# A weight decode whose low part is subtracted on GpSimd instead of TensorE and ScalarE, with a new table of issue times

## The chip, the cores and the metric

The kernel runs on one core of one Trainium2 chip. The metric is device time in microseconds (us) of one execution, from the launch to the last output. Five engines work on their own instruction streams, each in order: PE (TensorE, matrix products), DVE (VectorE, elementwise), ACT (ScalarE, activation functions and copies), POOL (GpSimd, elementwise here), and SP (SyncE), which only issues the DMA transfers. They wait for each other through semaphores.

## What is computed

Two layers, one behind the other. The first is a recurrent attention (an mLSTM) over 4 batches, 8 heads, 768 positions and a head size of 40:

```python
for t in range(S):
    m_new = np.maximum(f_gate[:, :, t] + m, i_gate[:, :, t])
    f_stab = np.exp(f_gate[:, :, t] + m - m_new)
    i_stab = np.exp(i_gate[:, :, t] - m_new)
    m = m_new
    C = f_stab[..., None, None] * C + i_stab[..., None, None] * np.einsum('bhd,bhe->bhde', vt, kt)
    n = f_stab[..., None] * n + i_stab[..., None] * kt
    h_tilde = np.einsum('bhde,bhe->bhd', C, qt)
    denom = np.maximum(np.abs(np.einsum('bhd,bhd->bh', n, qt)[..., None]), 1.0)
    y[:, :, t] = sigmoid(o_gate[:, :, t]) * h_tilde / denom
```

The second is a feed-forward layer on the 3072 tokens of 320 features: `h = x @ w_in`, `g = h * erf(softplus(h))`, `out = g @ w_out`, with 2048 hidden features. The two weight matrices reach the device as 64-bit floats.

## The kernel before

**Attention in chunks.** The 768 positions are cut into 6 chunks of 128, and each chunk of each batch is one of 24 steps (`attention(s)`, line 497). A step makes gate products on PE (L566, L568), their exponential on ACT (`dm`, L573), a causal mask of `dm` on POOL (`affine_select`, L577, 128x512), scores on PE (L586 or L589), their product with the mask on DVE (L600), outputs and state (L626, L629, L639, L645, L652), the division by the denominator (L666 to L669), a small copy on POOL that fills a third block of 128 columns (L672), and three transposes (L678). The result goes to `xh` (ACT, L687) and `xl` (DVE, L691): the high part that a single-pass float matmul keeps, and the rest.

**The feed-forward layer in groups.** `mlp(g)` (line 801) is called for 48 groups. Each has 32 "up" matmuls into `h` (L818), nine instructions on ACT (L828 to L859, and `gh`, L868), four on DVE (L851, L855, L863, and L873, which makes `gl`, what `gh` leaves over), and 24 "down" matmuls: 16 with `gh` (L887, L888) and 8 with `gl` (L890). Four groups belong to two steps. L873 is the last elementwise pass of a group, and the group's eight L890 read it.

**Weights.** They are not loaded as floats but decoded on the chip. `decode` (line 699) is called 26 times: 10 blocks of 128x512 from `w_in` (two of them, the tails, put together from rows 256 to 319) and 16 blocks of 128x320 from `w_out`. ACT takes the upper word of each 64-bit number (`val`, L707), DVE shifts and merges bits in three passes (`bits`, L712, L713, L715), ACT writes the high part `hi` (`wh` or `woh`, L720), and the low part is `val - hi`: PE makes the difference in PSUM with two matmuls against the identity and the negative identity (`dif`, L725 and L726), and ACT copies it to `wl` or `wol` (`lo`, L730). For the tails, `lo` ends with `done()`: four DMA issues (L775) that put its halves in place in `wh`. `val` lies in a pool named `moe` that has two buffers of the name `bits`, so the third decode waits until the first has read its `val` for the last time. `raw` words of `w_out` lie in the two buffers `parts`, three blocks in each.

**What sets the order.** Each unit of work (a step, a group, a decode, a load) has a start time, and each of its parts an offset, from tables at the top of the file. `plan` is sorted by start plus offset, and the parts are written out in that order. So the tables set the order in which each engine, the DMA queue of SP among them, gets its instructions. The numbers in them are only sort keys.

The difference that the change touches is made by these lines:

```python
@at('dif')
def _():
    v.z = ps_a.tile([128, 512], F32, name="pa")[:, 0:n]
    nc.tensor.matmul(v.z, ident, v.val, start=True, stop=False)
    nc.tensor.matmul(v.z, nident, hi(), start=False, stop=True)
@at('lo')
def _():
    nc.scalar.activation(lo(), v.z, AF.Copy)
```

Of the kernel before, what the change touches and what calls it, by code (L numbers as in the profile page):

```python
# [49 lines left out]
SETUP = {'setup': -653.6399, 'rhs0': -316.5197, 'rhs1': -7.8928, 'sel': -20.425}  # L50
GATE = {'load': -160.6071,
    'scan': -129.7377,
    'g': -118.9644,
    'sum': -85.9459,
    'exp': -69.3145,
    'part0': -64.8632,
    'part1': -57.829,
    'part2': -53.3066,
    'rhs': -44.557}
ATT_FIRST = {'load': -98.3436,  # L60
    'loadv': -167.9076,
    'khi': -0.958,
    'qhi': -84.1108,
    'klo': -36.0204,
    'qlo': -40.8927,
    'stk0': -106.1734,
    'stk1': -42.28,
    'rows': -205.5,
    'pe0': -204.9951,
    'pe1': -84.7223,  # L70
    'ex0': -104.2074,
    'ex1': -80.6796,
    'sel0': -99.9161,
    'sel1': -76.6928,
    'S0': -72.5713,
    'S1': -66.4977,
    'vg0': -86.1606,
    'vg1': -75.2945,
    'w0': -66.7387,
    'w1': -60.3516,  # L80
    'th': -51.6975,
    'pq': -84.6914,
    'qa': -69.7526,
    'ph0': -50.833,
    'ph1': -48.4014,
    'ph2': -41.1641,
    'ph3': -34.4417,
    'pk0': -76.6612,
    'pk1': -43.5318,
    'sa0': -34.523,  # L90
    'sa1': -33.2596,
    'sk0': -75.5148,
    'sk1': -41.374,
    'den': -25.7622,
    'yg': -25.29,
    'y': -21.6911,
    'tr': -15.7542,
    'xh': -3.4201,
    'xl': -0.3588}
ATT_NEXT = {'load': -108.5865,  # L100
    'loadv': -65.7264,
    'khi': -43.9486,
    'qhi': -36.8481,
    'klo': 33.0974,
    'qlo': 4.1048,
    'stk0': -62.7653,
    'stk1': 33.0459,
    'rows': -112.0,
    'pe0': -92.4353,
    'pe1': -82.6231,  # L110
    'ex0': -85.3469,
    'ex1': -74.7973,
    'sel0': -83.8594,
    'sel1': -59.1013,
    'S0': -64.4044,
    'S1': -29.3249,
    'vg0': -46.0099,
    'vg1': -19.402,
    'w0': -39.4592,
    'w1': -14.1493,  # L120
    'th': -41.0893,
    'pq': -109.6295,
    'qa': -38.5364,
    'ph0': -10.0541,
    'ph1': -6.3375,
    'ph2': 5.1946,
    'ph3': 6.4602,
    'pk0': -35.9301,
    'pk1': -7.3506,
    'sa0': 27.0234,  # L130
    'sa1': -6.4202,
    'sk0': -34.6458,
    'sk1': -0.3263,
    'den': 17.2106,
    'yg': 28.411,
    'y': 30.5578,
    'tr': 34.3008,
    'xh': 35.0968,
    'xl': 36.9102}
ATT = {'load': -38.0873,  # L140
    'loadv': -22.0289,
    'khi': -26.4131,
    'qhi': -24.304,
    'klo': -21.0673,
    'qlo': -20.9744,
    'stk0': -13.01,
    'stk1': -20.7116,
    'rows': -35.0,
    'pe0': -16.191,
    'pe1': -27.6979,  # L150
    'ex0': -14.5235,
    'ex1': -17.8549,
    'sel0': -13.8199,
    'sel1': -15.9236,
    'S0': -5.8456,
    'S1': -11.6692,
    'vg0': -8.7917,
    'vg1': -11.6286,
    'w0': -5.765,
    'w1': -10.6719,  # L160
    'th': -5.5334,
    'pq': -27.7455,
    'qa': -20.3849,
    'ph0': 1.4564,
    'ph1': 1.6614,
    'ph2': 2.8445,
    'ph3': 3.6732,
    'pk0': 6.9497,
    'pk1': -1.5624,
    'sa0': 7.8642,  # L170
    'sa1': 7.8309,
    'sk0': 10.4729,
    'sk1': 17.4327,
    'den': 7.2966,
    'yg': 10.4519,
    'y': 11.8501,
    'tr': 12.5049,
    'xh': 15.9467,
    'xl': 18.6409}
DEC = {'val': 5.0509, 'bits': 10.1649, 'hi': 15.9164, 'lo': 23.6056, 'dif': 16.8262}  # L180
MLP_FIRST = {'up0': -25.2675,
    'up1': -24.8742,
    'up2': -13.1693,
    'up3': -10.2026,
    'hb0': -14.0725,
    'a0': -9.4604,
    'hb1': -7.0234,
    'a1': -0.5942,
    'a2': 7.0246,
    'sq': 10.8333,  # L190
    'b': 13.8647,
    'ah': 14.2406,
    'ab': 17.9958,
    'w': 25.3005,
    'wh': 30.591,
    'gh': 34.499,
    'gl': 42.3954,
    'dn0': 37.1922,
    'dn1': 48.9497,
    'dn2': 59.2234,  # L200
    'dn3': 64.3577,
    'dn4': 42.875,
    'dn5': 45.5271,
    'dn6': 49.4724,
    'dn7': 59.5752,
    'o0': 36.8732,
    'o1': 34.0907}
MLP_NEXT = {'up0': -18.4874,
    'up1': -16.4563,
    'up2': -11.6119,  # L210
    'up3': -8.3726,
    'hb0': -3.5817,
    'a0': -3.1283,
    'hb1': 1.554,
    'a1': 4.6412,
    'a2': 9.7819,
    'sq': 14.1995,
    'b': 19.2975,
    'ah': 18.6881,
    'ab': 23.8216,  # L220
    'w': 27.514,
    'wh': 30.5244,
    'gh': 31.6065,
    'gl': 34.1835,
    'dn0': 38.7502,
    'dn1': 41.4674,
    'dn2': 41.7867,
    'dn3': 43.0183,
    'dn4': 38.1388,
    'dn5': 38.505,  # L230
    'dn6': 38.8279,
    'dn7': 41.0082,
    'o0': 45.1806,
    'o1': 52.9655}
MLP = {'up0': 10.8805,
    'up1': 11.4884,
    'up2': 11.8654,
    'up3': 11.9285,
    'hb0': 15.2244,
    'a0': 15.6598,  # L240
    'hb1': 17.0074,
    'a1': 18.439,
    'a2': 21.5715,
    'sq': 26.4364,
    'b': 28.2508,
    'ah': 28.025,
    'ab': 31.1556,
    'w': 32.9184,
    'wh': 36.5709,
    'gh': 37.7529,  # L250
    'gl': 40.6316,
    'dn0': 53.5649,
    'dn1': 53.9605,
    'dn2': 62.3419,
    'dn3': 63.3041,
    'dn4': 58.6761,
    'dn5': 59.5966,
    'dn6': 64.956,
    'dn7': 65.2067,
    'o0': 65.5077,  # L260
    'o1': 71.0278}
MLP_END = {'up0': 2.8495,
    'up1': 12.452,
    'up2': 10.3409,
    'up3': 12.5617,
    'hb0': 14.7709,
    'a0': 14.8932,
    'hb1': 15.2803,
    'a1': 16.0175,
    'a2': 20.7093,  # L270
    'sq': 21.7587,
    'b': 24.9917,
    'ah': 35.3148,
    'ab': 39.3943,
    'w': 173.4526,
    'wh': 195.2319,
    'gh': 199.4465,
    'gl': 241.5957,
    'dn0': 241.7219,
    'dn1': 242.5048,  # L280
    'dn2': 242.974,
    'dn3': 247.762,
    'dn4': 284.9153,
    'dn5': 289.8658,
    'dn6': 296.6226,
    'dn7': 298.2198,
    'o0': 286.1734,
    'o1': 303.1319}
LOAD = {(0, 0): -100.853,
    (0, 1): -70.8649,  # L290
    (0, 2): -90.992,
    (1, 0): -57.6292,
    (1, 1): -81.5688,
    (2, 0): -81.2243,
    (2, 1): -17.405,
    (1, 2): -88.4947,
    (3, 0): -100.0948,
    (3, 1): -81.2029,
    ('o', 0): -373.8392,
    ('o', 3): -372.7625,  # L300
    ('o', 6): -15.5809,
    ('o', 9): -74.0241,
    ('o', 12): -93.0868,
    ('o', 15): 54.2361}
DECODE = {('i', 0, 0): -96.6206,
    ('i', 0, 1): -36.809,
    ('t', 0): -70.3377,
# [675 lines left out]
```

## Time and profile before

| what | value |
|---|---|
| median of 3 runs | 543.33 us (537.8 to 544.72) |
| the profiled execution's own time | 542.79 us |
| its span, first to last instruction | 541.1 us |
| what lies around the span | 1.7 us |
| TensorE clock granted, mean | 0.987 of full speed |
| DMA | 58.85 MB, mean 109 GB/s |

A row of the page's list of groups gives line, engine, operation, output and inputs, their shapes, count, then busy time in us and the mean of one in ns, then the idle time of the engine just before them and what ended it. A row of the timeline gives start (us from the span's start), duration, engine and line; in square brackets the idle time before it and what ended it. A table of windows gives, for each stretch, the busy time of PE, PEld (weight loads), DVE, ACT and POOL with the number of instructions in brackets, then the granted clock, the DMA share and GB/s.

### The profile page before, as it was taken

Reading aid. Unit: us, or ns where it says so; the run is one execution under the profiler, and the core shown is the slowest. Engines: PE = TensorE matmul, PEld = TensorE weight load, DVE = VectorE, ACT = ScalarE, POOL = GpSimd, SP = SyncE. Lnnn points to the kernel's source line nnn. Section 1 sums busy time; section 2 is a strip of 40 time slices with the busy share of each in tenths; the row PEclk is TensorE's granted clock in tenths of the full one; section 3 lists DMA queues with packets and bytes.
Section 4 is the critical chain, followed back from the end, with each engine's and each line's share of the span. In section 5 each row is a group of like instructions: output and inputs, shape, how many; then the busy total and the mean of one; then the engine's idle time right before and its main releaser. Section 6 shows DMA issues by size and latency. Waiting matters only on the chain.

```text
span 541.1 us, 10846 instructions
## 1 busy us (share of the span) xinstructions
PE 521.8 (96%) x4086; PEld 491.9 (91%) x4086; DVE 435.9 (81%) x693; ACT 448.2 (83%) x714; POOL 92.4 (17%) x112
## 2 busy tenths in 40 slices
PE   3989999999899999999999999999999999999997
PEld 2757799899899999999999999999999999999986
DVE  5987899979788878888888898788898678776663
ACT  5776999989868978979878978878979889889993
POOL 3220001312211211211211211211211220200000
PEclk9996999999899999999999999999999999999999
DMA  8996114504504503404513504513504514400000
GB/s 272 276 324 214 40 34 134 153 27 144 150 2 152 165 25 124 150 16 152 155 35 116 157 17 138 166 38 106 167 8 135 162 44 137 140 1 26 0 25 24
DMA packets 28302, 58.85 MB, mean 109 GB/s; under 512 B 4156, under 2 KB 8764, under 8 KB 28252
## 3 DMA queue, kind: packets, MB, share of 16 engines
q1 hardware_dynamic: 28252, 58.18, 34.8%
q8 instruction: 32, 0.52, 0.4%
q14 instruction: 18, 0.15, 0.1%
HBM read 33.40 MB, written 3.93 MB: 69 GB/s over the span
## 4 chain that ended last, share of the span: by engine, by line
PE 84%; DMA 6%; DVE 4%; ACT 3%; issue 1%; SPq 1%; POOL 0%; DVEq 0%; ACTq 0%; POOLq 0%
PE h L818 32%; PE po L887 10%; PE po L890 10%; PE po L888 9%; PE pa L629 7%; DMA n<-in_w_in_dram 4%; PE pa L626 4%; PE pa L586 3%; PE pa L639 3%; PE pa L725 2%; DMA stk<-parts 2%; PE pa L566 2%; PE pa L678 1%; PE pa L589 1%; SPq L554 1%
## 5 line engine op out<-in xcount | busy, mean ns | idle before, releaser
L818 PE MATMUL h<-xh,wh 128*128 128x256 f32 x576 | 160.1, 287 | 0.0
L818 PE MATMUL h<-xl,wh 128*128 128x256 f32 x576 | 157.3, 282 | 0.0
L887 PE MATMUL po<-woh,gh 128*128 128x320 f32 x384 | 122.4, 330 | 2.1 <-ACT o_sb L896 1.3
L888 PE MATMUL po<-wol,gh 128*128 128x320 f32 x384 | 114.9, 310 | 0.0
L818 PEld LDWEIGHTS h<-xh,wh 128*128 128x128 f32 x576 | 109.6, 190 | 1.9 <-issue 1.0
L818 PEld LDWEIGHTS h<-xl,wh 128*128 128x128 f32 x576 | 109.5, 190 | 0.2
L818 PE MATMUL h<-xh,wl 128*128 128x256 f32 x384 | 108.3, 282 | 0.0
L873 DVE TENSOR_TENSOR gl<-hb,gh 128x1024 fp32r<-128x1024 f32 x48 | 59.7, 1243 | 21.8 <-ACT gh L868 16.6
L577 POOL TENSOR_SCALAR_AFFINE_SELECT dm<-dm 128x512 f32<-128x512 f32 x48 | 47.2, 985 | 170.2 <-ACT dm L573 162.2
L887 PEld LDWEIGHTS po<-woh,gh 128*128 128x128 f32 x384 | 72.8, 190 | 2.7 <-ACT o_sb L896 1.6
L868 ACT ACTIVATE gh<-hb 128x1024 fp32r<-128x1024 f32 x48 | 50.9, 1060 | 28.3 <-DVE hb L863 27.8
L888 PEld LDWEIGHTS po<-wol,gh 128*128 128x128 f32 x384 | 72.9, 190 | 0.6
L818 PEld LDWEIGHTS h<-xh,wl 128*128 128x128 f32 x384 | 73.0, 190 | 0.0
L890 PE MATMUL po<-woh,gl 128*128 128x320 f32 x384 | 72.6, 319 | 0.0
L855 DVE SCALAR_TENSOR_TENSOR n<-n,n 128x1024 f32<-128x1024 f32 x48 | 58.7, 1224 | 14.9 <-ACT n L847 12.2
L851 DVE SCALAR_TENSOR_TENSOR n<-n,hb 128x1024 f32<-128x1024 f32 x48 | 61.8, 1288 | 4.3 <-ACT n L842 4.2
L863 DVE SCALAR_TENSOR_TENSOR hb<-n,hb 128x1024 f32<-128x1024 f32 x48 | 58.4, 1217 | 7.6 <-ACT n L859 7.4
L828 ACT ACTIVATE hb<-h 128x512 f32<-128x512 f32 x96 | 57.3, 597 | 6.1 <-PE h L818 3.3
L859 ACT ACTIVATE n<-n 128x1024 f32<-128x1024 f32 x48 | 51.4, 1070 | 11.4 <-DVE n L855 11.3
L890 PEld LDWEIGHTS po<-woh,gl 128*128 128x128 f32 x384 | 58.9, 188 | 1.1
L834 ACT ACTIVATE n<-h 128x512 f32<-128x512 f32 x96 | 57.8, 602 | 0.0
L629 PE MATMUL pa<-kvo,dm 128*128 128x41 f32 x384 | 54.8, 273 | 0.0
(102 smaller groups left out, 896.4 us busy)
## 6 DMA issues: line engine op xcount, KB each, us to landing
stk<-parts SPq DMA_DIRECT2D x120, 160.0 KB
kvo<-in_kvo_dram SPq DMA_DIRECT2D x24, 484.0 KB
parts<-in_w_out_dram SPq DMA_DIRECT2D x5, 960.0 KB
parts<-in_qk_dram SPq DMA_DIRECT2D x20, 208.0 KB
q_t<-in_qk_dram SPq DMA_DIRECT2D x20, 208.0 KB
out_dram<-o_sb SPq DMA_DIRECT2D x24, 160.0 KB
stk<-in_qk_dram SPq DMA_DIRECT2D x4, 416.0 KB
hb<-in_w_in_dram SPq DMA_DIRECT2D x2, 512.0 KB
```

The costliest lines, as they stand in the source:

```text
L629: nc.tensor.matmul(v.ph[:, 2 * p + j], v.w[j][:, p], v.v1[:, 2 * p + j], start=(c == 0), stop=(c == 0 or j == 1))
L818: nc.tensor.matmul(v.h[n // 2][:, n % 2 * T:(n % 2 + 1) * T], w, m, start=(q == 0), stop=(q == len(ops) - 1))
L828: nc.scalar.activation(v.hb[:, hs], v.h[i], AF.Copy)
L834: nc.scalar.activation(v.a[:, hs], v.h[i], AF.Tanh, scale=PARAMS[0], bias=PARAMS[1])
L851: nc.vector.scalar_tensor_tensor(out=v.a, in0=v.a, scalar=PARAMS[8], in1=v.hb, op0=ALU.add, op1=ALU.mult)
L855: nc.vector.scalar_tensor_tensor(out=v.a, in0=v.a, scalar=PARAMS[9], in1=v.b, op0=ALU.mult, op1=ALU.add)
L859: nc.scalar.activation(v.a, v.a, AF.Tanh, scale=PARAMS[10], bias=PARAMS[11])
L863: nc.vector.scalar_tensor_tensor(out=v.hb, in0=v.a, scalar=1.0, in1=v.hb, op0=ALU.add, op1=ALU.mult)
L873: nc.vector.tensor_tensor(v.gl, v.hb, v.gh.bitcast(F32), op=ALU.subtract)
L887: nc.tensor.matmul(po[k, b], v.gh[:, ts], woh[:, w], start=(j == 0), stop=False)
L888: nc.tensor.matmul(po[k, b], v.gh[:, ts], wol[:, w], start=False, stop=False)
L890: nc.tensor.matmul(po[k, b], v.gl[:, ts], woh[:, w], start=False, stop=(j == NFF - 1))
```

## The change

In `decode` the part `dif` goes away. GpSimd subtracts `hi` from `val` and writes the low part straight to `wl`, `wol` or the tail's buffer; the negative identity and the PSUM tile are not needed any more. All tables of start times and offsets have new numbers.

```diff
@@ setup
         make_identity(nc, ident)
-        nc.scalar.activation(nident, ident, AF.Copy, scale=-1.0)
@@ decode
-        @at('dif')
-        def _():
-            v.z = ps_a.tile([128, 512], F32, name="pa")[:, 0:n]
-            nc.tensor.matmul(v.z, ident, v.val, start=True, stop=False)
-            nc.tensor.matmul(v.z, nident, hi(), start=False, stop=True)
-
         @at('lo')
         def _():
-            nc.scalar.activation(lo(), v.z, AF.Copy)
+            nc.gpsimd.tensor_tensor(lo(), v.val, hi().bitcast(F32), op=ALU.subtract)
             if done:
                 done()
@@ tables (every one of them has new numbers; two of their lines)
-DEC = {'val': 5.0509, 'bits': 10.1649, 'hi': 15.9164, 'lo': 23.6056, 'dif': 16.8262}
+DEC = {'val': 8.7894,
+    'bits': 10.5581,
+    'hi': 15.5618,
+    'lo': 22.9715}
```

Line numbers move by 4 above `decode` (L577 becomes L581) and by -2 behind it (L873 becomes L871); the subtraction is L728. In the rows below the engine's instructions stand in order, with output and inputs; `splB`, `spl` are gate rows, `dm` a step's mask, `kvo` its values and its result, `wol`, `woh` the low and high part of `w_out`, `wl`, `wh` those of `w_in`, `stk` the tails' buffer or a step's queries and keys, `bits` a decode's `val`.

POOL, from the first steps' gate rows on. Before:

```order
L559 COPY splB_81<-spl 32x256
L559 COPY splB_82<-spl 32x256
L577 AFFINE_SELECT dm<-dm 128x512 x4
L559 COPY splB_83<-spl 32x256
L559 COPY splB_84<-spl 32x256
L672 COPY kvo<-kvo 128x64
L577 AFFINE_SELECT dm<-dm 128x512 x2
```

POOL in the new order, a few decodes into the same stretch:

```order
L728 TENSOR_TENSOR wol<-bits,woh 128x320 x3
L676 COPY kvo<-kvo 128x64
L563 COPY splB_82<-spl 32x256
L563 COPY splB_83<-spl 32x256
L728 TENSOR_TENSOR wol<-bits,woh 128x320
L728 TENSOR_TENSOR stk<-bits,stk 128x512
L676 COPY kvo<-kvo 128x64
L728 TENSOR_TENSOR wl<-bits,wh 128x512 x2
L581 AFFINE_SELECT dm<-dm 128x512
```

The 26 subtractions stand among the masks and copies that the first steps need, on a queue that had only those.

DVE, the rows up to the third group's L873. Before:

```order
L691 TENSOR_TENSOR xl<-pa,xh 128x3x128
L851 SCALAR_TENSOR_TENSOR n_834<-n_834,hb 128x1024
L855 SCALAR_TENSOR_TENSOR n_834<-n_834,n_990 128x1024
L539 TENSOR_TENSOR parts<-parts 104x512
L547 TENSOR_TENSOR parts<-q_t,parts 104x512
L863 SCALAR_TENSOR_TENSOR hb<-n_834,hb 128x1024
L617 COPY aL<-pa 128x4
L618 TENSOR_TENSOR q_t<-q_t,pa 104x512
L873 TENSOR_TENSOR gl<-hb,gh 128x1024
```

DVE in the new order, up to the same instruction (L871 now):

```order
L716 TENSOR_SCALAR bits<-bits 128x320
L717 SCALAR_TENSOR_TENSOR bits<-parts,bits 128x320
L719 SCALAR_TENSOR_TENSOR bits<-parts,bits 128x320
L861 SCALAR_TENSOR_TENSOR hb<-n_752,hb 128x1024
L543 TENSOR_TENSOR parts<-parts 104x512
L551 TENSOR_TENSOR parts<-q_t,parts 104x512
L621 COPY aL<-pa 128x4
L622 TENSOR_TENSOR q_t<-q_t,pa 104x512
L871 TENSOR_TENSOR gl<-hb,gh 128x1024
```

The last decode has moved closer to it, but counted from the program's start the same instructions, kind for kind, stand ahead of the third group's `gl` in both orders. All 26 decodes are among them. On PE, from the first matmul that reads that `gl` to the end, the two orders have the same matmuls as well, but for two L887 and two L888 that the new order has already issued by then.

SP's DMA queue, some way into the loads of the weights (`gl`, `gh`, `n_...` are buffers that hold raw words of `w_in`, `parts` of `w_out`). Before:

```order
L748 DMA gl<-in_w_in_dram 128x1024
L788 DMA parts<-in_w_out_dram 128x3x640
L748 DMA n_328<-in_w_in_dram 128x1024
L519 DMA stk<-in_qk_dram 104x1024 x2
L748 DMA gh<-in_w_in_dram 128x1024
L775 DMA wh<-stk 64x512 x4
L429 DMA gt<-in_gates_dram 128x2x128
```

In the new order:

```order
L761 DMA n_220<-in_w_in_dram 64x1024 x2
L746 DMA n_223<-in_w_in_dram 128x1024
L746 DMA gl<-in_w_in_dram 128x1024
L746 DMA gh<-in_w_in_dram 128x1024
L746 DMA gl<-in_w_in_dram 128x1024
L523 DMA stk<-in_qk_dram 104x1024
L433 DMA gt<-in_gates_dram 128x2x128
L773 DMA wh<-stk 64x512 x4
L523 DMA stk<-in_qk_dram 104x1024
L786 DMA parts<-in_w_out_dram 128x3x640
L529 DMA kvo<-in_kvo_dram 128x968
```

The gates of the second chunk (`gt`) now stand ahead of the four issues that wait for the tail's low part, and behind these stand a step's queries and keys, three blocks of `w_out` and values.

More of the change, by code (lines that the diff above doesn't have):

```diff
@@ new lines @@
+ATT = {'load': -37.6545,
+    'loadv': -40.0461,
+    'khi': -23.1621,
+    'qhi': -21.9738,
+    'klo': -21.0462,
+    'qlo': -20.6645,
+    'stk0': -6.0689,
+    'stk1': -11.7104,
+    'rows': -49.5631,
+    'pe0': -21.7378,
+    'pe1': -35.0259,
+    'ex0': -15.8689,
+    'ex1': -33.2968,
+    'sel0': -14.0366,
+    'sel1': -17.9254,
+    'S0': -4.8028,
+    'S1': -7.5032,
+    'vg0': -7.8384,
+    'vg1': -7.7965,
+    'w0': -3.3309,
+    'w1': -6.7068,
+    'th': 2.1402,
+    'pq': -30.9768,
+    'qa': -17.9234,
+    'ph0': 3.6707,
+    'ph1': 5.9266,
+    'ph2': 3.8407,
+    'ph3': 4.9924,
+    'pk0': 6.9538,
+    'pk1': 6.931,
+    'sa0': 15.2353,
+    'sa1': 12.8128,
+    'sk0': 15.8865,
+    'sk1': 22.5476,
+    'den': 7.8787,
+    'yg': 8.4538,
+    'y': 11.0385,
+    'tr': 13.7023,
+    'xh': 17.0317,
+    'xl': 18.7594}
```

536 lines of the change are left out of this document (249 added, 287 removed).

## The prediction

> **What bounds the kernel now.** I read the page's busy times first, then a table of windows to see where which engine is short, then the timelines of DVE and PE where the start hands over to the even part.
>
> ```profile
> PE 521.8 (96%) x4086; PEld 491.9 (91%) x4086; DVE 435.9 (81%) x693; ACT 448.2 (83%) x714; POOL 92.4 (17%) x112
> ```
>
> ```profile
> 0.00:9.00 9.00, 0.31 (x1) 0.13 (x2) 4.03 (x13) 4.13 (x7) 3.70 (x18) 1.00 0.69 237
> 9.00:93.90 84.90, 82.69 (x532) 65.38 (x531) 71.87 (x141) 70.69 (x142) 10.44 (x17) 0.94 0.59 179
> 93.90:135.00 41.10, 39.90 (x335) 38.36 (x334) 37.80 (x59) 36.97 (x57) 10.33 (x9) 1.00 0.36 110
> 135.00:200.00 65.00, 63.18 (x511) 60.55 (x510) 53.32 (x87) 51.62 (x81) 14.11 (x13) 0.97 0.34 103
> 200.00:500.00 300.00, 300.00 (x2458) 292.62 (x2457) 247.23 (x378) 255.12 (x392) 53.87 (x56) 1.00 0.32 99
> 500.00:541.10 41.10, 35.72 (x258) 34.84 (x257) 21.69 (x19) 29.69 (x39) 0.00 (x0) 1.00 0.05 16
> ```
>
> The page says PE. The table says it with a limit: from 200 to 500 us PE has no idle time at all, while DVE has 53 of 300 us free; there PE alone counts. All decodes lie in the first 94 us, and there PE, DVE and ACT are all near full: DVE works 71.87 of 84.90 us, 85%. What PE saves there is only worth what DVE can follow.
>
> How closely DVE is followed, the third group's `gl` shows, the last one that has a decode ahead of it:
>
> ```profile
> 93.90 1.23 DVE L873 TENSOR_TENSOR gl<-hb,gh 128x1024 fp32r<-128x1024 f32 x1 [0.46 <-ACT gh L868]
> ```
>
> ```profile
> 95.07 0.31 PE L888 MATMUL po<-wol,gh 128*128 128x320 f32 x1
> 95.22 0.31 PE L887 MATMUL po<-woh,gh 128*128 128x320 f32 x1
> 96.69 0.45 PE L890 MATMUL po<-woh,gl 128*128 128x320 f32 x2
> ```
>
> `gl` is ready at 95.13, and the first matmul that reads it starts at 96.69: 1.6 us of slack. From that matmul on PE has the same work in both orders but for four matmuls, at 0.15 us each (the spacing of the first two rows) 0.6 us less. So if PE stays as full behind it as before, the span becomes 541.1 - 1.6 - 0.6 = 538.9 us plus the shift D of this `gl`. DVE has the same instructions ahead of it in both orders, so D has two terms: the time S that GpSimd's subtractions cost DVE, less the idle time I that DVE gets rid of.
>
> **What goes: PE and ACT work.** A pair of matmuls and its successor on PE:
>
> ```profile
> 27.67 0.79 PE L725 MATMUL pa<-bits,ident 128*128 128x320 f32 x2
> 28.05 0.55 PE L726 MATMUL pa<-woh,nident 128*128 128x320 f32 x1
> 28.44 0.42 PE L629 MATMUL pa<-kvo,dm 128*128 128x41 f32 x3
> ...
> 57.42 1.13 PE L725 MATMUL pa<-bits,ident 128*128 128x512 f32 x2
> 57.98 0.80 PE L726 MATMUL pa<-stk,nident 128*128 128x512 f32 x1
> 58.71 0.49 PE L589 MATMUL pa<-stk 40*128 40x128 f32 x2
> ```
>
> 0.77 us for 320 columns, 1.29 us for 512, start to next start: 16 x 0.77 + 10 x 1.29 = 25.2 us of PE. On ACT:
>
> ```profile
> L730 ACT ACTIVATE wol<-pa 128x320 fp32r<-128x320 f32 x16 | 7.0, 437 | 0.0
> L730 ACT ACTIVATE wl<-pa 128x512 fp32r<-128x512 f32 x8 | 4.7, 582 | 1.1 <-PE pa L726 1.1
> L730 ACT ACTIVATE stk<-pa 128x512 fp32r<-128x512 f32 x2 | 1.2, 589 | 0.0
> ```
>
> 12.9 us. Neither is taken off the end as it stands, since DVE's instructions ahead of the third `gl` remain. They come in through I.
>
> **I, the idle time DVE can lose.** From 9 to 93.9 us it is 84.90 - 71.87 = 13.0 us, of which the table of waits names
>
> ```profile
> DVE bits L712 <- ACT bits L707: 7.5, 8, 1.7
> DVE m_c L435 <- DMA gt<-in_gates_dram: 2.1, 1, 2.1
> DVE gl L873 <- ACT gh L868: 0.5, 1, 0.5
> DVE hb L863 <- ACT n L859: 0.3, 1, 0.3
> DVE n L851 <- ACT n L842: 0.2, 1, 0.2
> ```
>
> 10.6 us; the rest is small gaps. The gates' load moves ahead of the tail's four issues in SP's queue, so its 2.1 us should go: the lower end. Ten and a half is the upper end. The 7.5 us are waits for ACT to write the next `val`. ACT gets 12.9 us lighter, which helps; but a `val` buffer (two of them) is now freed by POOL, whose queue also holds masks and copies that wait for ACT and DVE, and the next decode stands behind that. I take half of the 7.5 with the 2.1: I = 6.
>
> **S, what the subtractions cost DVE.** The trace has no two-input POOL instruction. The nearest row is the mask, one input of 512 elements:
>
> ```profile
> L577 POOL TENSOR_SCALAR_AFFINE_SELECT dm<-dm x48: 636/1032/1501, 10.5 to 470.3; 128x512 f32<-128x512 f32 x48
> ```
>
> ```profile
> 40.22 0.64 POOL L577 TENSOR_SCALAR_AFFINE_SELECT dm<-dm 128x512 f32<-128x512 f32 x1 [1.85 <-ACT dm L573]
> ```
>
> ```profile
> 40.40 1.00 DVE L715 SCALAR_TENSOR_TENSOR bits<-n,bits 128x512 int32<-128x512 int32 x1
> ...
> 42.97 0.69 DVE L715 SCALAR_TENSOR_TENSOR bits<-gl,bits 128x512 int32<-128x512 int32 x1
> ```
>
> The same DVE instruction takes 0.69 us alone and 1.00 us when a mask of 0.64 us has just started: the mask took 0.31 us of it. DVE's decode passes and group passes also read two operands from SBUF, so nearly all it does in this stretch can be hit; that it can gain is excluded. Lower end: a subtraction costs no more than a mask per column, 0.31 us for 512, 0.19 for 320: 10 x 0.31 + 16 x 0.19 = 6.1, times the 0.85 of the time that DVE works, 5.2 us. Upper end: DVE is held for the subtraction's whole time, and two inputs take twice the mask's: 1.28 and 0.80 us, 25.6 us, times 0.85 is 21.8. I take the row as it reads, 0.31 us per 512 elements read, with two inputs read: 0.62 and 0.39 us, 12.4 us in all, times 0.85: S = 10.5.
>
> The Trainium skill, GPSIMD Engine Reference, section 3.1, gives 4497 ns for a tensor_tensor over 2048 floats on GpSimd, by which a subtraction of 512 would take some 1.12 us and one of 320 some 0.70, an estimate; no run here shows it yet, and it says nothing of what DVE loses.
>
> **Other engines and the queues.** POOL gets at most 25.6 us more in 94 us, beside 14.1 us of its own, so it isn't full. What queues behind a subtraction there: masks (DVE's L600 waits for them), gate rows (PE's first products) and the copy ahead of the transposes. On SP, the tail's four issues wait for its low part, and behind them stand a step's queries and keys, three blocks of `w_out` and values; before it was the same queue behind ACT:
>
> ```profile
> SPq L775 <- ACT wl L730: 13.0, 1, 13.0
> ```
>
> A wait of 13.0 us there went with full DMA engines, so I cost it at nothing; were the cover gone, the decodes of those blocks would be late, and that is DVE's idle time, within the bounds of I. The tail of the program has the same PE work behind the last "up" matmul, and I cost it at nothing.
>
> **Sum.** D = 10.5 - 6 = 4.5; span 538.9 + 4.5 = 543.4; with 1.7 us around it 545 us, against 542.8 for the profiled execution and a median of 543.3. So no change that a measurement can tell. By the bounds: D from 5.2 - 10.6 = -5.4 to 21.8 - 2.1 = 19.7, that is 535 to 560 us.
>
> **Rivals.** *DVE isn't held, and its waits go:* the subtractions fall into its gaps, S is 0, I is 10.6, D = -10.6: 530 us, faster. For it: ACT is the named cause of most waits and loses 12.9 us. Against it: the waits and the collisions must both vanish at 85% load. The extreme of it, PE setting the end everywhere, would be 542.8 - 25.2 = 518; the 71.87 us of DVE work that stay forbid it.
>
> *DVE is held for all of a subtraction:* S = 21.8, and with I = 6 D is 15.8: 556 us, slower. It decides from S above I + 13.6, where the loss passes 2%. For it: the mask's 0.31 us is what a DVE instruction lost that came 0.18 us after the mask's start, so the hold may be longer than what is seen. Against it: the mask ran 0.18 + 0.31 = 0.49 us until DVE got on, less than its 0.64. The Trainium skill, SBUF — State Buffer, section "SBUF: two separate sides", has this rule: a DVE instruction with two SBUF inputs and a GpSimd instruction that reads SBUF lock the shared ports for the whole instruction, and the other blocks fully. By that rule this rival would hold; the row agrees on the blocking and not quite on its length.
>
> *The new order leaves gaps later:* if the idle time of 135 to 200 us, 1.82 of 65 us, went on to 500, that is 2.8% of 300 us, 8.4 us, and 545 becomes 554. For it: every table has new numbers; against it: PE has the same work there, and DVE 18% free.
>
> **How the numbers follow.** The forecast, 0.62; DVE not held, 0.15; held throughout, 0.17; gaps later, 0.06. A measurement of this kernel can tell about 2% from no change, that is outside 532.5 to 554.2 us. Faster is the second case, 0.15; slower the third and half of the fourth, 0.20; same the rest, 0.65. The predicted time is 545 us. The range takes in the bounds of the sum and most of the second case: 531 to 560.
>
> **What would show it.** Right: the third `gl` starts between 90 and 103 us; DVE's L717, L719 and the group passes show several rows 0.3 to 0.7 us longer than alone; DVE works over 90% of the time ahead of that `gl`; PE is full from 200 to 500 us. Wrong: PE at work without gaps from its first "up" matmul on and a third `gl` ahead of 85 us (the second case), DVE rows that are 0.8 us and more too long (the third), or idle time of PE behind 200 us (the fourth). If `gl` moves and the end doesn't follow it, the slack that I read from two rows isn't the bound.

## The result and the profile after

The changed kernel takes **548.51 us** (median of 4 runs, 548.09 to 549.06). The kernel before took 541.83 us on the same chip. The ratio is 1.0145 with a 95% interval of 1.0101 to 1.019: slower, by less than 2%. The profiled execution took 548.3 us, its span is 546.6 us, 5.5 us longer than before. The profiled executions lie within 2 us of their kernels' medians, but that of experiment 8 is 4.7 us above its median, so the waits in it may not be typical of that kernel.

The page's busy times after:

```profile
PE 508.2 (93%) x4008; PEld 487.7 (89%) x4008; DVE 455.4 (83%) x693; ACT 439.2 (80%) x687; POOL 140.1 (26%) x138
```

PE has lost 78 matmuls and DVE has not gained an instruction, but DVE is busy 19.5 us longer. Where, the table of windows of the changed kernel says, cut at the start of the third, tenth and 38th group's `gl`:

```profile
9.00:103.97 94.97, 73.52 (x464) 64.68 (x465) 86.63 (x140) 61.15 (x116) 40.81 (x44) 0.93 0.54 163
...
103.97:179.06 75.09, 71.53 (x588) 69.07 (x587) 64.22 (x104) 62.55 (x98) 16.56 (x17) 0.95 0.32 101
179.06:459.54 280.48, 280.48 (x2331) 272.41 (x2329) 242.19 (x376) 238.84 (x365) 72.40 (x56) 1.00 0.35 105
459.54:546.60 87.06, 82.70 (x633) 81.57 (x631) 58.41 (x64) 73.13 (x105) 7.08 (x5) 1.00 0.15 47
```

The same groups in the kernel before:

```profile
93.90:166.63 72.73, 69.71 (x570) 66.75 (x569) 62.60 (x103) 59.58 (x93) 16.53 (x15) 0.98 0.32 97
166.63:449.52 282.89, 282.89 (x2330) 274.66 (x2329) 237.80 (x376) 238.83 (x367) 56.50 (x58) 1.00 0.34 105
449.52:541.10 91.58, 86.20 (x661) 84.97 (x659) 59.64 (x64) 74.99 (x108) 5.27 (x7) 1.00 0.17 52
```

So the 5.5 us are a sum with both signs: +10.07 us up to the third `gl` (93.90 to 103.97), +2.36 to the tenth, -2.41 over the 28 groups behind it, and -4.52 to the end. Over the 28 groups PE has no idle time in either kernel and the same number of matmuls within one, yet needs 2.4 us less. (Some expectations below call such a stretch 32 groups; it was measured from the ninth to the 37th `gl`, which is 28.) The second and the last of the four terms partly belong together: the changed kernel has 18 matmuls more between the third and the tenth `gl` and 28 fewer in the last stretch. Of DVE's 19.5 us, 14.8 lie ahead of the third `gl`; 4.4 lie in the 28 groups, where PE is never idle.

The third `gl`, and the first readers of the second and of the third, in the timelines of DVE and of PE after:

```profile
103.97 1.22 DVE L871 TENSOR_TENSOR gl<-hb,gh 128x1024 fp32r<-128x1024 f32 x1
```

```profile
97.72 1.45 PE L888 MATMUL po<-woh,gl 128*128 128x320 f32 x8 [1.59 <-DVE gl L871]
...
106.19 1.04 PE L888 MATMUL po<-woh,gl 128*128 128x320 f32 x6
```

The third `gl` is ready at 103.97 + 1.22 = 105.19, and its reader starts at 106.19: of the 1.6 us of slack 1.0 is still there. PE waited 1.59 us for the second group's `gl`, and from 97.72 to the third one's reader its timeline shows no idle time.

Ahead of the third `gl` DVE works 86.63 of 94.97 us, 91%: S = 86.63 - 71.87 = 14.76 us of work more, for one instruction fewer in the window. Its idle time is 8.34 us where it was 13.03, so I = 4.69. How an instruction grows, the timeline shows (DVE and POOL rows of the changed kernel):

```profile
31.43 0.49 DVE L719 SCALAR_TENSOR_TENSOR bits<-parts,bits 128x320 int32<-128x320 int32 x1
...
32.50 0.90 POOL L728 TENSOR_TENSOR wol<-bits,woh 128x320 fp32r<-128x320 f32 x1 [2.85 <-ACT woh L724]
32.72 1.03 DVE L719 SCALAR_TENSOR_TENSOR bits<-parts,bits 128x320 int32<-128x320 int32 x1
...
44.30 0.69 DVE L717 SCALAR_TENSOR_TENSOR bits<-gh,bits 128x512 int32<-128x512 int32 x1
44.68 1.44 POOL L728 TENSOR_TENSOR wl<-bits,wh 128x512 fp32r<-128x512 f32 x1 [2.10 <-ACT wh L724]
45.03 1.64 DVE L719 SCALAR_TENSOR_TENSOR bits<-gh,bits 128x512 int32<-128x512 int32 x1
```

A pass of 320 takes 0.49 us alone and 1.03 beside a subtraction, one of 512 takes 0.69 alone and 1.64. Taking its own time off its end, the first got on at 32.72 + 1.03 - 0.49 = 33.26 us, the second at 45.03 + 1.64 - 0.69 = 45.98; the subtractions end at 33.40 and 46.12. Both times DVE stands still until 0.14 us before the subtraction's recorded end. Nine of the decodes' two-operand passes in this trace (L717, L719) start while a subtraction runs, and the same working gives 0.14 or 0.15 us for all nine; the passes are 0.54 to 1.06 us longer than alone. That holds for the mask of the kernel before as well: it ended at 40.86, and the pass behind it got on at 40.40 + 1.00 - 0.69 = 40.71.

Not every DVE instruction stands still:

```profile
23.07 0.86 POOL L728 TENSOR_TENSOR wol<-bits,woh 128x320 fp32r<-128x320 f32 x1
23.27 0.69 DVE L604 TENSOR_TENSOR dm<-pa,dm 128x512 f32<-128x512 f32 x1
```

This one reads one operand from PSUM (`pa`), runs in the middle of a subtraction, and takes its 0.69 us. In the groups from 9 to 103.97 us:

```profile
L719 DVE SCALAR_TENSOR_TENSOR bits<-parts,bits 128x320 int32<-128x320 int32 x16 | 10.7, 670 | 0.5
...
L604 DVE TENSOR_TENSOR dm<-pa,dm 128x512 f32<-128x512 f32 x8 | 5.3, 686 | 0.3
...
L728 POOL TENSOR_TENSOR wol<-bits,woh 128x320 fp32r<-128x320 f32 x15 | 14.2, 945 | 24.1 <-ACT woh L724 24.0
L728 POOL TENSOR_TENSOR wl<-bits,wh 128x512 fp32r<-128x512 f32 x8 | 11.0, 1369 | 16.1 <-ACT wh L724 13.5 <-ACT den L661 1.3 <-DMA hb<-in_w_in_dram 1.3
L728 POOL TENSOR_TENSOR stk<-bits,stk 128x512 fp32r<-128x512 f32 x2 | 2.9, 1438 | 1.4 <-issue 1.3
```

L604, with its PSUM operand, has a mean of 686 ns, where it was 683 before. L719, with two operands in SBUF, has 670 ns over 16 instead of 490. The 25 subtractions in this window take 28.1 us of POOL, and DVE lost 14.8.

DVE's waits in the same stretch:

```profile
DVE bits L716 <- ACT bits L711: 2.7, 4, 0.9
DVE vg L599 <- POOL dm L581: 2.6, 1, 2.6
DVE den L670 <- ACT den L661: 0.5, 2, 0.2
```

ACT's `val` is down from 7.5 to 2.7 us, the wait for the gates' load is gone, and a new one has come: a mask, 2.6 us. The subtraction ahead of it on POOL's queue isn't what makes it late: in experiment 7 POOL has no subtraction, has been idle for 7.1 us when it starts the same masks, and DVE waits 2.7 us for them. In both kernels ACT writes that step's `dm` only from 15.9 or 16.1 us on.

### The profile page after: what moved, and what is told of

Its sections match the earlier page's. It is cut to its first block, busy times and chain, and to the rows that moved or that the text cites. A ratio compares the mean times of both kernels' runs of the same rounds, so it can differ in the third digit from the quotient of the medians.

```text
span 546.6 us, 10570 instructions
## 1 busy us (share of the span) xinstructions
PE 508.2 (93%) x4008; PEld 487.7 (89%) x4008; DVE 455.4 (83%) x693; ACT 439.2 (80%) x687; POOL 140.1 (26%) x138
## 3 DMA queue, kind: packets, MB, share of 16 engines
HBM read 33.40 MB, written 3.93 MB: 68 GB/s over the span
## 4 chain that ended last, share of the span: by engine, by line
PE 75%; DVE 15%; ACT 4%; issue 3%; DMA 1%; SPq 1%; POOL 0%; DVEq 0%; ACTq 0%; POOLq 0%
PE h L816 30%; PE po L885 9%; PE po L888 9%; PE po L886 9%; PE pa L633 6%; PE pa L590 3%; PE pa L630 3%; DVE bits L717 3%; DVE bits L719 3%; PE pa L643 2%; DVE bits L716 2%; PE pa L570 1%; PE pa L682 1%; DVE n L849 1%; DVE n L853 1%
## 5 line engine op out<-in xcount | busy, mean ns | idle before, releaser
L816 PE MATMUL h<-xh,wh 128*128 128x256 f32 x576 | 163.9, 292 | 0.3 <-ACT hb L826 0.3
L816 PE MATMUL h<-xl,wh 128*128 128x256 f32 x576 | 159.8, 284 | 0.0
L816 PEld LDWEIGHTS h<-xh,wh 128*128 128x128 f32 x576 | 111.2, 193 | 1.6 <-ACT hb L826 0.5
L816 PEld LDWEIGHTS h<-xl,wh 128*128 128x128 f32 x576 | 111.1, 193 | 0.4 <-DVE xl L695 0.3
L581 POOL TENSOR_SCALAR_AFFINE_SELECT dm<-dm 128x512 f32<-128x512 f32 x48 | 61.1, 1284 | 167.2 <-ACT dm L577 160.3
L888 PE MATMUL po<-woh,gl 128*128 128x320 f32 x384 | 83.3, 322 | 1.6 <-DVE gl L871 1.6
L633 PE MATMUL pa<-kvo,dm 128*128 128x41 f32 x384 | 62.0, 297 | 8.1 <-DVE dm L604 7.3
L633 PEld LDWEIGHTS pa<-kvo,dm 128*128 128x128 f32 x384 | 56.6, 214 | 9.4 <-DVE dm L604 7.9
L853 DVE SCALAR_TENSOR_TENSOR n<-n,n 128x1024 f32<-128x1024 f32 x48 | 62.3, 1298 | 1.5 <-ACT n L845 0.5
L888 PEld LDWEIGHTS po<-woh,gl 128*128 128x128 f32 x384 | 61.2, 189 | 2.5 <-DVE gl L871 1.9
L871 DVE TENSOR_TENSOR gl<-hb,gh 128x1024 fp32r<-128x1024 f32 x48 | 59.1, 1232 | 2.4 <-ACT gh L866 2.4
```

The costliest lines, as they stand in the source:

```text
L581: nc.gpsimd.affine_select(out=v.w[j], in_=v.w[j], pattern=[[0, NPR], [1, L]], compare_op=ALU.is_ge, fill=0.0, base=0, channel_multiplier=-1)
L633: nc.tensor.matmul(v.ph[:, 2 * p + j], v.w[j][:, p], v.v1[:, 2 * p + j], start=(c == 0), stop=(c == 0 or j == 1))
L816: nc.tensor.matmul(v.h[n // 2][:, n % 2 * T:(n % 2 + 1) * T], w, m, start=(q == 0), stop=(q == len(ops) - 1))
L853: nc.vector.scalar_tensor_tensor(out=v.a, in0=v.a, scalar=PARAMS[9], in1=v.b, op0=ALU.mult, op1=ALU.add)
L871: nc.vector.tensor_tensor(v.gl, v.hb, v.gh.bitcast(F32), op=ALU.subtract)
L888: nc.tensor.matmul(po[k, b], v.gl[:, ts], woh[:, w], start=False, stop=(j == NFF - 1))
```

## Experiments

Three questions: does the held DVE set the end of the start; what were PE's and ACT's 25 and 13 us worth; and where do the 4.6 us behind the third `gl` come from? "DVE work" below is from 9 us to the third `gl`.

| kernel | DVE work | DVE idle | third `gl` | from it to the end | median us | ratio to before (95%) |
|---|---|---|---|---|---|---|
| before | 71.87 | 13.03 | 93.90 | 447.2 | 540.74 to 541.83 | 1 |
| changed | 86.63 | 8.34 | 103.97 | 442.6 | 548.51 | 1.0145 (1.0101 to 1.019) |
| old order, GpSimd | 86.86 | 9.16 | 105.02 | 448.0 | 554.32 | 1.0263 (1.0218 to 1.0308) |
| subtraction on DVE | 84.28 | 9.29 | 102.57 | 440.9 | 546.32 | 1.0118 (1.0074 to 1.0162) |
| half a subtraction | 77.93 | 9.18 | 96.11 | 442.7 | 540.4 | 0.9999 (0.9976 to 1.0021) |
| low part by ACT | 72.32 | 16.58 | 97.90 | 441.8 | 542.25 | 1.0024 (0.9998 to 1.005) |
| twice the subtraction | 102.28 | 8.45 | 119.73 | 442.8 | 564.24 | 1.0422 (1.0364 to 1.048) |
| zeros, new order | 73.54 | 11.42 | 93.96 | 441.8 | 539.42 | 0.9961 (0.9931 to 0.9991) |
| zeros, old order | 73.71 | 6.35 | 89.06 | 449.2 | 541.06 | 0.9988 (0.9965 to 1.0011) |
| new tables behind the start | 72.07 | 14.82 | 95.89 | 443.9 | 542.39 | 1.0033 (0.9994 to 1.0072) |
| old tables behind the start | 86.36 | 8.35 | 103.71 | 463.8 | 569.17 | 1.0499 (1.0435 to 1.0564) |
| new tables, later seam | 72.87 | 10.75 | 92.62 | 438.8 | 533.71 | 0.9866 (0.9838 to 0.9894) |
| GpSimd for `w_out` alone | 78.07 | 32.77 | 119.84 | 442.6 | 559.45 | 1.0307 (1.0261 to 1.0353) |

**1. The subtraction in the old order.** All tables as before, `dif` taken out.

```diff
-        @at('dif')
-        def _():
-            v.z = ps_a.tile([128, 512], F32, name="pa")[:, 0:n]
-            nc.tensor.matmul(v.z, ident, v.val, start=True, stop=False)
-            nc.tensor.matmul(v.z, nident, hi(), start=False, stop=True)
-            nc.scalar.activation(lo(), v.z, AF.Copy)
+            nc.gpsimd.tensor_tensor(lo(), v.val, hi().bitcast(F32), op=ALU.subtract)
```

> The order of the kernel before, with the two identity matmuls and the copy replaced by GpSimd's subtraction: the subtraction alone. Port theory (each subtraction holds back a DVE instruction for its own duration less about 0.32 us, 15 us in all ahead of the third group's low part): DVE's busy time up to that instruction goes from 76 to about 90 us, the instruction from 93.9 to 102 to 106, and the time to 548 to 553 us. Order theory (the new order is what costs time, the subtraction is free): 538 to 543 us.

554.32 us, slightly above what the port's theory allows, and far from the rival's. The subtraction costs DVE the same, 86.86 - 71.87 = 14.99 us, in an order that was not made for it. The new order did not make the loss; it takes 1.2% off it, and the table shows that this comes mostly behind the third `gl`, 442.6 instead of 448.0 us.

**2. The subtraction on DVE itself.** New order; `lo` placed at once behind `hi`.

```diff
-    'lo': 22.9715}
+    'lo': 18}
-            nc.gpsimd.tensor_tensor(lo(), v.val, hi().bitcast(F32), op=ALU.subtract)
+            nc.vector.tensor_tensor(lo(), v.val, hi().bitcast(F32), op=ALU.subtract)
```

> The new order with the subtraction on DVE, 2.5 time units after the high part, GpSimd without it. DVE gets 16 passes of 0.49 and 10 of 0.69 us as work, 14.7 us, and loses the stalls. Port theory: 14.7 us of work for some 15 us of stalls, so the same time within 1%, 544 to 553 us, and the decode's third bit pass back to 0.49 and 0.69 us. If the stalls cost nothing on the path, the added work comes on top: 556 to 563 us.

546.32 us. The groups of DVE up to 110 us:

```profile
L728 DVE TENSOR_TENSOR wol<-bits,woh 128x320 fp32r<-128x320 f32 x16 | 8.2, 513 | 3.1 <-ACT woh L724 3.1
...
L728 DVE TENSOR_TENSOR wl<-bits,wh 128x512 fp32r<-128x512 f32 x8 | 5.5, 686 | 0.2
...
L728 DVE TENSOR_TENSOR stk<-bits,stk 128x512 fp32r<-128x512 f32 x2 | 1.4, 682 | 0.0
```

DVE does all 26 itself in passes that sum to 15.1 us. In the table's measure, busy time ahead of the third `gl`, they add 84.28 - 71.87 = 12.4 us (records of neighbouring passes overlap a little), and GpSimd's subtractions cost DVE 14.8. The two ratios' intervals overlap: handing the work over saved DVE nothing.

**3. Half a subtraction.** The second half of the columns gets zeros.

```diff
-            nc.gpsimd.tensor_tensor(lo(), v.val, hi().bitcast(F32), op=ALU.subtract)
+            m = n // 2
+            nc.gpsimd.memset(lo().bitcast(F32)[:, m:n], 0.0)
+            nc.gpsimd.tensor_tensor(lo()[:, 0:m], v.val[:, 0:m], hi().bitcast(F32)[:, 0:m], op=ALU.subtract)
```

> The new order; GpSimd subtracts the first half of each block's columns and writes zeros into the other half, so half of the low parts is left out. Port theory: a subtraction takes some 0.48 and 0.68 us, holds DVE 0.16 and 0.36 us, 5 us in all in place of 15; third low part near 95 us, time 538 to 544 us. Order theory: 546 to 549 us as in the changed kernel.

```profile
9.00:96.11 87.11, 72.59 (x464) 64.36 (x465) 77.93 (x141) 60.30 (x116) 36.70 (x69) 0.92 0.59 178
```

540.4 us, as the port's theory expected: S falls to 6.06 us, and the third `gl` comes 7.9 us earlier, although POOL has 25 instructions more.

**4. Twice the subtraction.**

```diff
-            nc.gpsimd.tensor_tensor(lo(), v.val, hi().bitcast(F32), op=ALU.subtract)
+            for _ in range(2):
+                nc.gpsimd.tensor_tensor(lo(), v.val, hi().bitcast(F32), op=ALU.subtract)
```

> The changed kernel, with each of the 26 subtractions done twice on GpSimd, the second writing the same result again. Theory of the port (each subtraction holds DVE for its own length less about 0.3 us): half a subtraction cost DVE 6.1 us ahead of the third group's gl and a whole one 14.8, so a second one adds 9 to 15; the third gl starts at 113 to 119 us and the time is 557 to 564 us. Rival, that the start is set by its order of issue and by POOL's queue and not by DVE's held passes: POOL has 54 us free in that stretch and takes the second pass in it, so the third gl stays within 4 us of 104 and the time is 548 to 552 us.

```profile
9.00:119.73 110.73, 76.23 (x468) 66.59 (x469) 102.28 (x141) 62.42 (x116) 70.28 (x68) 0.89 0.45 139
```

564.24 us, a hair above the port's theory and far from the rival's. S is 30.41 us: half, whole and twice give 6.1, 14.8 and 30.4. POOL is still idle for 40 us in that window; it is DVE that is full, with 8.45 us idle. What DVE loses goes into the end nearly one to one: 15.6 us more of S, 15.8 us on the third `gl`, 15.7 on the time.

**5. Zeros in place of the subtraction.** POOL keeps an instruction at each place, one that reads nothing.

```diff
-            nc.gpsimd.tensor_tensor(lo(), v.val, hi().bitcast(F32), op=ALU.subtract)
+            nc.gpsimd.memset(lo().bitcast(F32), 0.0)
```

> The changed kernel with the subtraction left out: GpSimd writes zeros to every low part in its place, so POOL's queue keeps an instruction at each of the 26 places, but one that reads no operand. Theory of the port: DVE is not held, its work ahead of the third gl is back at 72 to 73 us; idle time there was 8.3 to 9.2 us in the three kernels in which neither PE nor ACT makes the low part; so the third gl starts at 89.5 to 91.5 us and the time is 532 to 535 us. Rival, that the new order of issue has a later start of its own, whatever makes the low part (with ACT copies in its place and no held passes it was 97.9): third gl at 95 to 99 us, time 538.5 to 543 us.

```profile
9.00:93.96 84.96, 71.01 (x465) 63.48 (x466) 73.54 (x140) 59.90 (x116) 22.52 (x44) 0.94 0.60 182
```

539.42 us: the time is the rival's, and the third `gl`, at 93.96, lies between the two. DVE's work is nearly back, as the port's theory says (73.54), but it idles 11.42 us and not 8 to 9. The 1.7 us that its work is still above before lie mostly in passes with one operand: L716 over 512 columns has a mean of 529 ns, where it was 423 (L712 before). What follows is a third thing: 25 us less PE work and 13 us less ACT work, at a price of 1.7 us on DVE, leave the third `gl` in the new order where it was before, within 0.1 us.

**6. Zeros in the old order.** The same edit, in the kernel before, with `dif` taken out.

> The old tables, difference on PE and ACT left out, subtraction left out as well: GpSimd writes zeros to the low parts. So PE is 25 and ACT 13 us lighter, and DVE is not held. With the new tables the same left the third gl at 93.96 us, where it was before. Theory, that PE's and ACT's work ahead of the third gl was cover and not bound: here too it stays within 3 us of 93.9, and behind it the old tables take 447 to 448 us; time 540 to 545 us. Rival, that it is worth what the forecast's I says or more (6 to 10.6 us of DVE's idle time): third gl at 83 to 88 us, time 532 to 537 us.

```profile
9.00:89.06 80.06, 67.81 (x463) 59.88 (x461) 73.71 (x140) 60.94 (x116) 19.84 (x43) 0.81 0.64 190
```

Here `gl` does come 4.8 us earlier, between the two expectations, with I = 13.03 - 6.35 = 6.7 us; but the stretch behind takes 449.2 us, 2 us more than before, and the time, 541.06 us, cannot be told from before (0.9965 to 1.0011). Even a difference that costs PE and ACT nothing, and DVE 1.8 us, gains no time that can be measured in the old order. Set beside experiment 5, it also shows that the new start on its own is later: with zeros in both, its third `gl` comes 4.9 us behind the old one's (93.96 and 89.06), as the rival there had it.

PE's part is not without any effect, though. Of the 55 executions of the kernel before that were timed beside the experiments, the four with a mean granted clock of 1.000 took 537.5 to 538.8 us and the eight at 0.987 took 542.1 to 543.8; the zeros in the old order took 540.1 and 541.1 at 0.964 and 0.965, and 539.5 at 0.997. With PE's part in the start the time goes with the clock, and without it these runs show no such trend.

**7. The low part by ACT.** New order; the subtraction is left out, and ACT copies `val` right behind `hi`.

```diff
-    'lo': 22.9715}
+    'lo': 16}
-            nc.gpsimd.tensor_tensor(lo(), v.val, hi().bitcast(F32), op=ALU.subtract)
+            nc.scalar.activation(lo(), v.val, AF.Copy)
```

> The new order with no subtraction at all: ACT copies the value into the low part right behind the high part, so the low parts are left out as differences, PE and GpSimd have no part in the decode, and ACT has the 13 us of copies it had before. Port theory: DVE's stalls of 15 us go, third low part near 90 us, time 532 to 539 us. Order theory: 545 to 549 us.

542.25 us; both theories missed. The held time is gone (72.32 us of work, S = 0.45), but DVE waits instead: 16.58 us of idle time take the place of 8.34. From its waits up to 100 us:

```profile
DVE bits L716 <- ACT bits L711: 5.7, 9, 1.3
DVE vg L599 <- POOL dm L581: 2.7, 1, 2.7
```

The wait for ACT's next `val`, which now stands behind its copies, is 5.7 us for 2.7 in the changed kernel; the mask's is 2.7 for 2.6; the rest is spread over the gates' load (1.5 us) and small waits for ACT and PE. So in this start DVE can be late in two ways: held by GpSimd, or waiting for others, an ACT that makes the low parts the largest of them.

**8. GpSimd for `w_out` alone.** New order; the ten blocks of `w_in` get PE's and ACT's difference back.

```diff
+        @at('dif')
+        def _():
+            if name[0] == 'o':
+                return
+            v.z = ps_a.tile([128, 512], F32, name="pa")[:, 0:n]
+            nc.tensor.matmul(v.z, ident, v.val, start=True, stop=False)
+            nc.tensor.matmul(v.z, nident, hi(), start=False, stop=True)
...
-            nc.gpsimd.tensor_tensor(lo(), v.val, hi().bitcast(F32), op=ALU.subtract)
+            if name[0] != 'o':
+                nc.scalar.activation(lo(), v.z, AF.Copy)
+            else:
+                nc.gpsimd.tensor_tensor(lo(), v.val, hi().bitcast(F32), op=ALU.subtract)
```

> The changed kernel, with the difference of the 10 blocks of w_in made by PE and ACT again and only the 16 blocks of w_out subtracted on GpSimd. Theory of the port: 16 subtractions of 0.86 us are 13.8 of the 26.5 us that all 26 take alone, so DVE's held time falls from 14.8 to 7 to 8 us; with 9 to 11 us of idle time the third gl starts at 96 to 99 us and the time is 540 to 543 us. Rival, that PE's and ACT's work being gone was what kept the start short: 12.9 us more for PE and 5.9 for ACT make the third gl no earlier than 102 us and the time 546 us or more.

559.45 us, and a third `gl` at 119.84: a miss for the port's time, and inside what the rival named. The port's count came near: S = 78.07 - 71.87 = 6.2 us for 7 to 8. The idle time did not, 32.77 us in the profiled execution, whose granted clock in this stretch was 0.83. DVE's waits from 9 to 120 us:

```profile
DVE bits L719 <- ACT bits L714: 15.0, 10, 2.6
DVE bits L719 <- PE pa L575: 6.3, 1, 6.3
DVE hb L875 <- ACT n L871: 5.6, 1, 5.6
```

So in the new order PE's and ACT's part, put back, is far from worth nothing. A likely reading is that an order worked out without that part has no place for it, so that PE and ACT reach it in turn and DVE waits behind them; whether the place or the work itself costs the time, this run does not tell.

**9. Which tables make the gain behind the start.** First the tables ATT, MLP, MLP_END, GROUP_EVERY, STEP_BEFORE and CHUNK_BEFORE were exchanged whole, in the kernel before (the new ones in) and in the changed one (the old ones in).

```diff
@@ the kernel before (the other way round in the changed one)
-GROUP_EVERY = 13.6151
-STEP_BEFORE = (26.1425, 14.2715)
-CHUNK_BEFORE = -5.1551
+GROUP_EVERY = 13.706
+STEP_BEFORE = (25.4535, 12.3912)
+CHUNK_BEFORE = 1.4159
```

> The kernel before with its own difference on PE and ACT and its own tables for the start; only the tables of the even part and the end (ATT, MLP, MLP_END, GROUP_EVERY, STEP_BEFORE, CHUNK_BEFORE) are the new ones. From the third gl to the end the kernels with the new tables took 441 to 443 us, those with the old ones 447 to 448. Theory, that this gain lies in the even part and the end, where PE does the same 2342 matmuls of 32 groups in 281.0 instead of 283.7 us and the last groups in 3.5 us less: third gl at 93.9 us as before, time 536 to 539 us. Rival, that the gain is what the new start leaves done when it ends: time 541 to 544 us, as before.

> The mirror image: the changed kernel with GpSimd's subtraction and the new tables for the start, but the old tables for the even part and the end. Theory, that the gain behind the third gl lies in the even part and the end: third gl at 104 us, time 551 to 555 us. Rival, that the gain comes with the new start: 547 to 550 us.

542.39 us, which the rival named, and 569.17 us, which neither did: the theory missed in both. From the third `gl` to the end the two took 443.9 and 463.8 us, where whole sets take 442.6 and 447.2. The stretch behind the 38th `gl` has the new order's gain in the first of them (87.5 us), but its third `gl` is 2 us later than before: the seam costs about what was to be seen. So the exchange was made again, with a later seam: the old tables for the first six steps, nine groups and two chunks of gates, the new ones behind.

```diff
-    return ATT_FIRST if s < 2 else ATT_NEXT if s < 4 else ATT
+    return ATT_FIRST if s < 2 else ATT_NEXT if s < 4 else ATT if s < 6 else ATT2
-    return MLP_FIRST if g < 1 else MLP_NEXT if g < 4 else MLP if g < 46 else MLP_END
+    return MLP_FIRST if g < 1 else MLP_NEXT if g < 4 else MLP if g < 9 else MLP2 if g < 46 else MLP_END
-        at = unit(chunk_at(c), GATE)
+        at = unit(chunk_at(c), GATE if c < 2 else GATE2)
```

> The kernel before (difference on PE and ACT, its own tables) up to the fifth step and eighth group; from the seventh step, the tenth group and the third chunk of gates on, and in the last groups, the new tables. In the exchange of tables that ran first, the fifth and sixth step and the groups from the fifth on had new offsets while the start around them was old (2 us lost at the third gl), and the gates kept the old table (41.1 us for every second four groups, as before, where the changed kernel takes 40.45). Theory, that the gain of the new order is PE's pace in the even part and in the last groups: third gl at 93.9 us, 32 groups in 281 instead of 283.7 us, 86 instead of 89.4 us from there to the last gl, span 534.5 to 537 us, time 536 to 539 us. Rival, that the gain needs the new start, or that a seam between tables always costs what it brings: 540 to 544 us.

The windows, cut at the third, tenth and 38th `gl`:

```profile
9.00:92.62 83.62, 80.61 (x543) 64.49 (x542) 72.87 (x144) 71.41 (x142) 11.58 (x17) 0.98 0.60 183
92.62:163.53 70.91, 69.00 (x581) 66.75 (x580) 63.20 (x101) 62.25 (x96) 18.86 (x17) 1.00 0.35 106
163.53:444.27 280.74, 280.74 (x2336) 272.73 (x2336) 242.29 (x377) 239.53 (x367) 72.77 (x56) 1.00 0.34 106
444.27:531.40 87.13, 82.68 (x633) 81.55 (x631) 58.40 (x64) 73.20 (x105) 7.07 (x5) 1.00 0.15 47
```

533.71 us (533.04 to 536.71), better than expected, and faster than both kernels: 0.9866 of before. Against the changed kernel it is 0.9866 / 1.0145 = 0.972. Its 28 groups take 280.74 us, as in the changed kernel (280.48) and not as before (282.89); its end 87.13, as there (87.06) and not 91.58. The other kernels bear it out: the same 28 groups take 282.9 to 284.1 us in the three with the old tables throughout, and 280.4 to 280.7 in the seven with the new ones. So the larger part of the gain, 6.6 of the 9.7 us between the two profiled executions, lies in the even part and the last groups, and it needs no GpSimd: here PE and ACT make the difference. The other 3.1 us lie ahead of the tenth `gl`, where the granted clock differs too (0.98 and 1.00, before 0.94 and 0.98), so they are not the tables' alone.

How a full PE gains time, the timelines show in part. The state products `vg,kvo`, 192 in the 28 groups, stand in 24 runs of eight before, and in 12 runs of 16 with the new tables. Two places of PE's timeline, before and after:

```profile
234.06 0.51 PE L890 MATMUL po<-woh,gl 128*128 128x320 f32 x2
234.50 0.50 PE L639 MATMUL pa<-vg,kvo 128*40 128x41 f32 x8
234.93 1.15 PE L890 MATMUL po<-woh,gl 128*128 128x320 f32 x6
```

```profile
254.12 0.64 PE L888 MATMUL po<-woh,gl 128*128 128x320 f32 x2
254.69 0.97 PE L643 MATMUL pa<-vg,kvo 128*40 128x41 f32 x16
255.59 0.38 PE L816 MATMUL h<-xh,wh 128*128 128x256 f32 x1
```

From its start to the next matmul a run of eight takes 0.43 us, and one of 16 takes 0.62 to 0.90, 0.76 in the mean, not twice 0.43. The matmul ahead of a run keeps PE for 0.23 us, where a `po` matmul ahead of another takes 0.15. Twelve runs fewer are then 12 x (0.10 + 0.08) = 2.2 of the 2.4 us, an estimate from these spacings. No run changes this alone, and it isn't all: the first exchange of tables has twelve runs too, and its 28 groups took 282.4 us, 0.4 of it idle.

## Why the prediction came out as it did

The time, 548.5 us for 545, lies in the range, and the class (no change that 2% can tell) is the forecast's. Several steps under it were off, and their errors partly cancel.

**The frame held in front, not behind.** The third `gl` moved by S - I as the sum put it: 14.76 - 4.69 = 10.07. It lies at 103.97, 1 us outside the 90 to 103 that I named; DVE works 91% of the time ahead of it (over 90% named), and PE is full from 200 to 500 us. With twice the subtraction the end followed S almost one to one. But "if PE stays as full behind it as before" hid an assumption: that a full PE with the same matmuls has the same pace. It needed 2.4 us less for 28 groups, and 4.5 less in the last stretch (with 28 fewer matmuls left there, and less idle time: 91.58 - 86.20 = 5.38 against 4.36 us); 2.4 us of that went again between the third and the tenth group, where 18 matmuls more were done. By the sum the span should have been 538.9 + 10.07 = 549.0; it is 546.6. Two errors make up the 2.4 us: the sum took all of the 1.6 us of slack off, and 1.0 stayed; and from the first reader of the third `gl` to the end PE took 440.4 us for 444.4, which is 3.4 us less when the 0.6 for four matmuls is counted off. The longer runs of state products are a likely part of that pace (experiment 9); the rest stays open. With S and I as measured my sum would have said 551 us, so that the forecast of 545 came within 3.5 us of the result is luck in part: no step of it had PE's pace.

**S was mis-sized: 14.8, not 10.5 us.** The step that failed is the reading of the mask's row. A pass that came 0.18 us late lost 0.31 us of a mask of 0.64, and I scaled those 0.31 as if they were the hold. The hold was 0.49 us, from the mask's start to 0.15 before its end, and the same rows say so. The subtractions hold in the same way, 0.14 us short of their own time: 0.72 us for one of 0.86, 1.13 for one of 1.27. For the 25 that lie ahead of the third `gl` that is 15 x 0.72 + 10 x 1.13 = 22.1 us if every microsecond met a DVE pass that has to wait. It cost 14.8, 67%: passes with a PSUM operand run on, passes already under way when a subtraction comes lose nothing by it, and DVE is idle at times; how the missing third divides among these was not measured. My own sign of the third case came, too: DVE rows 0.8 us and more too long. Of the nine passes that started while a subtraction ran, the four that met one of 512 columns were 0.94 to 1.06 us longer than alone. The upper bound of 21.8 was the right mechanism, and the third case held it; what was measured lies 0.38 of the way from the forecast's 10.5 to it. The Trainium skill, SBUF — State Buffer, section "SBUF: two separate sides", which says that whoever of the two comes first has the shared ports for its whole instruction and the other blocks fully, agrees with these rows to 0.14 us; I had taken the mask's row against it.

**I was near: 4.69 for 6.** The gates' 2.1 us went as forecast, ACT's 7.5 fell to 2.7. (Where DVE isn't held, 1.5 us of the gates' wait are there in the new order as well, experiment 7: the place in SP's queue alone does not remove it.) What I left out is a wait that the new order brings, 2.6 us for a mask, with subtractions on POOL or without. I also depends on S and on the order: with no hold it was 6.7 us in the old order and 1.6 in the new, with the whole subtraction 3.9 and 4.7. It is not a term of its own; why the two orders differ in it, the runs do not show.

**PE's 25.2 and ACT's 12.9 us.** "Neither is taken off the end as it stands" held, and more strongly than I put it: with both gone and zeros in place of the subtraction, the new order's third `gl` moved by 0.06 us; the old order's came 4.8 us earlier, but its time changed by nothing that can be measured.

**The rivals.** *DVE isn't held* is out: the rows show it, and so do four doses from zeros to twice. *Held throughout* is right on the mechanism and too high in the sum, since a third of the held time meets nothing that has to wait. *The new order leaves gaps later* is out: PE has no idle time from 200 to 500 us, and behind the third `gl` the new order took 4.6 us less, by PE's pace more than by gaps. That is also why the change as a whole reads as 1.5% and not as the 2.6% that the subtraction alone costs in the old order.

## What to carry to other kernels

Before work is moved to GpSimd, look at what DVE runs beside it: if those are passes with two operands in SBUF, count GpSimd's own time as DVE's, less what meets no such pass; here 28 us on GpSimd cost DVE at least as much as doing the work itself. Work that is taken from an engine that is full beside another full one can be worth nothing, and a kernel that simply leaves it out shows that in one run. When a change comes with a new order of issue, run the order without the change: here the order of the even part and the end was the gain and the change the loss.

## What the runs showed of the hardware

- A two-operand DVE pass in SBUF waits for a GpSimd subtraction or mask until 0.14 to 0.15 us before its recorded end (nine passes behind a subtraction in the changed kernel, and the mask's row before); a pass of the same size with one operand in PSUM does not wait (0.69 us in the middle of a subtraction, mean 686 ns over 8).
- GpSimd's subtraction takes 0.86 us for 128x320 and 1.27 us for 128x512 where DVE doesn't hold it up; the figure of the Trainium skill, GPSIMD Engine Reference, section 3.1 (4497 ns for 2048 floats), scaled to these sizes, gives an estimate of 0.70 and 1.12. It waits too: 1.44 us where it started 0.38 us into a DVE pass of 0.69.
- A full PE is not a fixed pace: 2330 matmuls in 282.89 us before and 2331 in 280.48 after, both without idle time and at a granted clock of 1.00. A run of eight matmuls of 41 columns takes 0.43 us to the next matmul, one of 16 takes 0.76 in the mean.
